# Forgetting attention and a tanh-shrink MLP on one core: batch 0's scores in two-bank groups, a selector tile, and unread matmuls in slot 1

## The chip, the cores and the metric

The kernel runs on one core of one Trainium2 chip. The metric is the device time of one execution in microseconds (us), the median over the runs shown. Engines are named as in the profile: PE (TensorE matmul), PEld (its weight load), DVE (VectorE), ACT (ScalarE), POOL (GpSimd), SP (SyncE, which here only issues DMAs).

## The reference

Causal attention with a forget gate for 8 batches of 8 heads (576 tokens, head width 64), then an MLP on the 4608 tokens of width 512, with hidden width 2048:

```python
scores = scale * np.matmul(q, k.transpose(0, 1, 3, 2))
log_f = np.log(np.clip(f, 0.0001, 1.0))
cum = np.cumsum(log_f, axis=-1)
decay = cum[:, :, :, None] - cum[:, :, None, :]
scores = np.where(causal, -1000000000.0, scores + decay)
attn = softmax(scores)            # max, exp, sum + 1e-09
x = matmul(attn, v)               # heads side by side: (4608, 512)
h = x @ w_in
return (h - np.tanh(h)) @ w_out
```

## The kernel before

**Pairs and slots.** Attention goes by pairs of heads, four pairs to a batch, 32 in all. A slot is the work around one pair: the scores of that pair, the values of the pair before it, the transposes of q and k of the next pair. Scores stand with the key tile on the partitions, so that they are `QT`/`KT` products and need no transpose. A head's scores are three tiles of up to 512 columns (a PSUM bank); the two heads share a small fourth one, tile 3. Head 0 has tiles 0, 1, 2 and head 1 has tiles 4, 5, 6. `GROUPS` names tiles that share a two-bank buffer and one exponential: group 0 is tiles 0 and 1, group 1 is tiles 2 and 4, group 2 is tiles 5 and 6, group 3 is tile 3.

**Decay.** `QT` and `KT` have 64 rows of data and three rows more: the running sum of log f enters the score matmul through these rows, which DMAs on SP's queue fill (`load_aug`, `const_rows`). Head 0 of batch 0 comes before these DMAs land, and so has its sums by selectors: two extra matmuls, one with `pick[:, 0:1]` (minus one at the two rows of head 0 in `cc`), one with `pick[:, 1:2]` against `cqs`. The code calls such a tile `direct`. A causal edge is one more matmul of 128 columns (`neg16`, `tri16`) in batch 0 and the first pair of batch 1; later an affine select on POOL.

**Order of the work.** All five engines run in the order in which the code issues their instructions. The first five slots follow hand-written lists (`FIRST`). A list's words: a bare number is so many `spin` matmuls of 512 columns into a bank that nobody reads; `q`/`k` with a number are six transposes of the q or k of the pair so many ahead, and the copies of them into `QT`/`KT`; `s` is one score tile, `g` a group; `va`/`vb` are the values of the two heads of the pair before (30 matmuls; after `vb` DVE computes the reciprocals and `xn`); `y` and `x` turn a finished `xn` into `XR` (five transposes on PE and one DVE copy in batch 0, DMA transposes later); `p` and `r` are DVE memsets of paddings (`pads`, `later_rows`; the second also issues DMAs); `h` and `m` are the first MLP steps; `c` issues DMAs.

**PSUM.** While the slots of batch 0 run, the eight banks are: two for `av` (values, and the unread matmuls), one `tr` and one `t2`, which the transposes of q, k and x take in turn (`t_bank`: odd calls `t2`, even calls `tr`), and four for scores: four buffers of one bank in slot 0, then two buffers of two banks. From slot 4 on there are `av`, `tr`, two score banks and three MLP banks.

**Later slots.** From slot 5 on, `att_items` lists a slot's tiles 0 to 6 with what goes between them (loads, transposes of the next pair behind tile 2 and tile 5, values of the pair before behind tile 1), and MLP steps are spread evenly among them. An MLP step of the first kind is four matmuls, a tanh on ACT and an add on DVE (`gt`, line 417, at times with two `sm` adds); of the second kind it is eight matmuls of a product of seven (a Strassen-like scheme, so that `wsum` forms differences of `w_out`'s blocks on DVE, `WT1` to `WT4`). For 512 tokens there are 16 of the first and 14 of the second. The transposes' copies run on DVE ("VV"), in slots 7 and 8 on ACT ("AA").

Of the kernel before, what the change touches and what calls it, by code (L numbers as in the profile page):

```python
# [8 lines left out]
FP32 = mybir.dt.float32  # L9
# [8 lines left out]
FAR = 3  # L18
# [4 lines left out]
def kernel(  # L23
# [104 lines left out]
    tri16 = WS[3].rearrange("p k e -> p (k e)")[:, 640:768]  # L128
    ones16 = cst.tile([P, S], FP16)
    minus16 = WS[2].rearrange("p k e -> p (k e)")[0:2 * H, 0:S]  # L130
    pick = cst.tile([P, 2], FP16)
    cc = cst.tile([P, S], FP16)
    chi, clo = cc[0:NH, :], cc[NH:2 * NH, :]
    cqs = cst.tile([P, S], FP16)
# [29 lines left out]
    nc.vector.memset(neg16, 0.0)  # L164
    nc.vector.memset(tri16, 0.0)
    nc.vector.memset(QT[0][D:D + 3, 0, :], 0.0)
    load_qk(qn, q, 0, 4, 6)
    load_qk(kn, k, 0, 4, 6)
    nc.gpsimd.affine_select(out=neg16, in_=neg16, compare_op=ALU.not_equal,
# [109 lines left out]
    def trans(b, c, src, dst, engs):  # L279
        pn, g3 = S // NT6, NT6 // 2  # L280
        t16 = t_bank().bitcast(FP16)[:, 0:2 * S // 2].rearrange("p (a g n) -> p a g n", a=2, g=g3)
        for a in range(2):
            for g in range(g3):
                nc.tensor.transpose(out=t16[:, a, g, :], in_=src[b % 2][:, 2 * c + a, 2 * g:2 * g + 2, :],  # L284
                                    identity=id16[0:pn, 0:pn])
        for a0, an in ((0, 1), (1, 1)) if len(engs) > 2 else ((0, 2),):
            for e in range(2):
                h0 = 2 * c + a0
                to = dst[b % 2][0:D, h0:h0 + an, 0:S].rearrange("d a (g e p) -> d a g e p", g=g3, e=2)[:, :, :, e, :]
                of = t16[e * D:(e + 1) * D, a0:a0 + an, :, :]  # L290
                if engs[2 * a0 + e] == "A":
                    nc.scalar.activation(out=to, in_=of, func=AF.Copy)
                else:
                    nc.vector.tensor_copy(out=to, in_=of)  # L294
            if a0 == 0 and engs == "AAAA":
                cum_q()

    def head_tiles(a):
        return [[(a, 0, 0, 512, 0)],
# [12 lines left out]
    def scores(b, c, tis, how):  # L312
        n2 = len(tis)
        banks = POOLS["s"].tile([P, 2 if how == "group" else 1, UW], FP32, tag="sc", name="ps")
        if tis[0] == LAST:
            eb = EL[(b * NPAIR + c) % 3].rearrange("p (o w) -> p o w", o=1)
        else:
            g, o = PLACE[tis[0]]
            if b == 0:
                if o == 0:  # L320
                    EB[(b, c, g)] = gtp.tile([P, 2, UW], FP16, tag="gt", name="e2")
                eb = EB[(b, c, g)][:, o:o + n2, :]
            else:
                eb = aex.tile([P, 1, UW], FP16, tag="e", name="e")
        for i, ti in enumerate(tis):
            ps, e = banks[:, i, :], eb[:, i, :]
            for a, j, i0, n, col in TILES[ti]:
                h = 2 * c + a
                edge = min(P, n) if how != "late" and i0 == j * P else 0
                direct = b == 0 and h == 0  # L330
                kn_ = min(P, S - j * P) if direct else P
                nc.tensor.matmul(out=ps[:, col:col + n], lhsT=KT[b % 2][0:D + 3, h, j * P:(j + 1) * P],  # L332
                                 rhs=QT[b % 2][0:D + 3, h, i0:i0 + n], start=True, stop=not (edge or direct))
                if direct:
                    nc.tensor.matmul(out=ps[0:kn_, col:col + n], lhsT=cc[:, j * P:j * P + kn_],
                                     rhs=pick[:, 0:1].to_broadcast([P, n]), start=False, stop=False)
                    nc.tensor.matmul(out=ps[:, col:col + n], lhsT=pick[:, 1:2].to_broadcast([P, P]),
                                     rhs=cqs[:, i0:i0 + n], start=False, stop=not edge)
                if edge:
                    nc.tensor.matmul(out=ps[:, col:col + edge], lhsT=neg16, rhs=tri16[:, 0:edge],  # L340
                                     start=False, stop=True)
# [6 lines left out]
        nc.scalar.activation(out=eb[:, :, lo:hi], in_=banks[:, 0:n2, lo:hi], func=AF.Exp, scale=qscale)  # L348
# [141 lines left out]
    for u in range(NU):  # L490
        mlp += [[(mlp1, u, ft)] for ft in turns]
        mlp += [[(product, u, n, g)] for n, g in ((1, 0), (1, 1), (2, 0), (6, 0), (6, 1), (2, 1))]
        mlp += [[(product, u, n, g)] for n in (5, 7, 3, 4) for g in range(2)]
    for at, n in ((NFT, 0), (NFT + 1, 2), (NFT + 3, 1), (NFT + 5, 3)):
        mlp[at] += [(wsum, n, 0, K2 // 2), (wsum, n, K2 // 2, K2)]

    STEPS = [0]

    def step():
        for fn, *args in mlp[STEPS[0]]:  # L500
            fn(*args)
        STEPS[0] += 1

    FIRST = [["8", "q0", "k0", "5", "s0", "s1", "q1", "s2", "k1", "p", "s4", "s5", "q2", "s6", "s3"],
# [4 lines left out]

    def first_slot(p):  # L510
        here = pairs[p]
        before = pairs[p - 1] if p else None
        for what in FIRST[p]:
            kind, arg = what[0], what[1:]
            if what == "m":
                step()
            elif kind == "h":
                mlp1_part(0, turns[int(arg)], 0, NCH - 1)
            elif kind == "s":
                scores(*here, (int(arg),), "one")  # L520
            elif kind == "g":
                scores(*here, GROUPS[int(arg)], "group")
            elif kind in "qk":
                trans(*pairs[p + int(arg)], *((qn, QT) if kind == "q" else (kn, KT)),
                      "VV" if p or arg != "0" else "AAAA" if kind == "q" else "VVVV")
                if what == "k0":
                    load_aug(0, 1)
            elif kind == "v":
                values(*before, 0 if arg == "a" else 1)
            elif kind == "r":  # L530
                later_rows()
            elif kind == "p":
                pads()
            elif kind == "c":
                const_rows(0, 0, 1)
                load_aug(2)
            elif kind == "x":
                turn(*before)
            elif kind == "y":
                turn(*pairs[p - 2])  # L540
            else:
                spin(int(what))

    def att_items(p):
# [67 lines left out]
```

## Time and profile before

| what | us |
|---|---|
| median of 3 runs | 350.78 (350.43 to 350.84) |
| the profiled execution, its own time | 350.38 |
| its span in the profile | 348.7 |
| PE busy | 334.7 |
| DVE busy | 253.3 |
| ACT busy | 220.2 |
| POOL busy | 176.9 |

The profile shows one execution. A row of the timeline has the start, the duration, the engine, the line, the operation, the tiles with shapes, the count, and in brackets how long the engine had been idle before it and what released it. A row of the windows has the stretch, its length, then the busy time and number of instructions of each engine, then the TensorE clock that was granted (1.00 is full speed), the DMA share and GB/s. Matmul durations include the way through the array, so that successive matmuls overlap: the spacing of starts is what a matmul costs.

### The profile page before, as it was taken

How to read it: one execution, taken by the hardware profiler on the slowest of the kernel's cores; microseconds unless marked ns; L12 is line 12 of the kernel's file. 1: busy time of each engine (PE TensorE's matmuls, PEld its weight loads, DVE VectorE, ACT ScalarE, POOL GpSimd, SP SyncE). 2: the span in 40 equal slices, each digit the busy share in tenths (PEclk: the TensorE clock that was granted, in tenths of full speed). 3: DMA queues.
4: the chain of work that ended last, by engine and by line, in shares of the span. 5: the costliest groups of instructions: out<-in, count | busy, mean ns of one | idle time of the engine just before them, and what ended most of it. 6: DMA issues, size and time to landing. Idle time of an engine off the chain costs nothing.

```text
span 348.7 us, 8658 instructions
## 1 busy us (share of the span) xinstructions
PE 334.7 (96%) x3295; PEld 234.1 (67%) x3295; DVE 253.3 (73%) x523; ACT 220.2 (63%) x412; POOL 176.9 (51%) x322
## 2 busy tenths in 40 slices
PE   7898998998999999999999999999999999999996
PEld 2585556774578656887886568756887786487475
DVE  7576889819896589748984889388937863873872
ACT  6564876777765786568756875588558843623631
POOL 8967179875277726774667457753222220500500
PEclk9989999999999999999999999999999999999999
DMA  9999999999589998999699979994122013003003
GB/s 100 145 181 176 195 180 136 131 168 208 83 65 119 179 149 80 116 168 175 65 120 141 180 87 110 156 168 74 47 83 46 19 34 122 0 12 111 3 0 122
DMA packets 169560, 38.82 MB, mean 111 GB/s; under 512 B 155906, under 2 KB 169454, under 8 KB 169518
## 3 DMA queue, kind: packets, MB, share of 16 engines
q0 software_dynamic: 116576, 18.36, 87.2%
q1 hardware_dynamic: 52942, 19.90, 29.1%
q8 instruction: 26, 0.43, 0.6%
q14 instruction: 16, 0.13, 0.1%
HBM read 36.85 MB, written 9.44 MB: 133 GB/s over the span
## 4 chain that ended last, share of the span: by engine, by line
PE 78%; DVE 12%; DMA 4%; ACT 3%; issue 2%; SPq 1%; POOL 0%; DVEq 0%; ACTq 0%; POOLq 0%
PE mb L404 29%; PE px L452 16%; PE mb L452 12%; PE ps L332 11%; PE av L369 7%; DVE gt L417 4%; DMA out_dram<-ost 2%; DVE KT L294 2%; DVE sm L431 2%; DVE xn L377 1%; DMA kn<-in_k_dram 1%; ACT th L411 1%; ACT e L348 1%; PE t L284 1%; DVE QT L294 1%
## 5 line engine op out<-in xcount | busy, mean ns | idle before, releaser
L404 PE MATMUL mb<-XR,win 128*128 128x512 f16 (+4 forms) x704 | 141.6, 340 | 1.0 <-DVE gt L417 0.7
L348 ACT ACTIVATE e<-ps 128x512 f16<-128x512 f32 (+1 forms) x183 | 109.3, 617 | 28.2 <-PE ps L332 15.7
L411 ACT ACTIVATE th<-mb 128x512 f32<-128x512 f32 x144 | 86.3, 600 | 50.8 <-PE mb L404 46.5
L417 DVE TENSOR_TENSOR gt<-mb,th 128x512 f16<-128x512 f32 x144 | 97.1, 686 | 25.2 <-ACT th L411 24.4
L359 POOL TENSOR_SCALAR_AFFINE_SELECT e<-e 128x128 f16<-128x128 f16 x162 | 59.7, 372 | 104.5 <-ACT e L348 103.9
L404 PEld LDWEIGHTS <-win 128*128 128x128 f16 x704 | 61.8, 97 | 49.2 <-issue 2.8
L332 PE MATMUL ps<-QT,KT 67*128 67x64 f16 (+4 forms) x384 | 75.4, 279 | 4.3 <-DVE KT L294 1.4
L452 PEld LDWEIGHTS <-gt 128*128 128x128 f16 x576 | 53.8, 97 | 10.9 <-DVE gt L417 1.1
L332 PEld LDWEIGHTS <-KT 67*128 67x128 f16 x384 | 36.3, 99 | 26.4 <-DVE KT L294 3.4
L452 PEld LDWEIGHTS <-sm 128*128 128x128 f16 x432 | 40.4, 97 | 7.2 <-DVE ws L266 0.6
L452 PE MATMUL mb<-ws,gt 128*128 128x256 f16 x288 | 36.4, 272 | 0.0
L482 DVE TENSOR_TENSOR ost<-mb,part 128x512 f32<-128x512 f32 x25 | 17.1, 685 | 25.9 <-PE mb L404 6.8
L369 PEld LDWEIGHTS <-e 128*128 128x128 f16 x896 | 32.9, 98 | 3.7 <-DVE xn L377 0.9
L369 PE MATMUL av<-vn,e 128*128 128x65 f16 x896 | 34.4, 194 | 0.7 <-DVE xn L377 0.7
L469 ACT ACTIVATE part<-px 128x512 f32<-128x512 f32 x24 | 14.3, 597 | 30.1 <-PE px L452 30.1
L452 PE MATMUL px<-ws,sm 128*128 128x256 f16 x256 | 31.6, 272 | 0.0
L113 POOL DMA_DIRECT2D vn<-in_v_dram x32 | 28.7, 905 | 2.4 <-issue 1.9
L377 DVE TENSOR_TENSOR xn<-av,rs 128x640 f16<-128x640 f32 x32 | 26.4, 824 | 1.1
L431 POOL TENSOR_TENSOR sm<-gt 128x512 f16<-128x512 f16 x4 | 4.6, 1152 | 36.3 <-DVE gt L417 36.3
L94 POOL DMA_DIRECT2D qn<-in_q_dram x25 | 21.8, 872 | 1.5 <-issue 1.4
L94 POOL DMA_DIRECT2D kn<-in_k_dram x25 | 21.4, 854 | 1.2 <-issue 0.9
L452 PE MATMUL mb<-wout,gt 128*128 128x256 f16 x160 | 21.4, 272 | 0.0
(83 smaller groups left out, 302.6 us busy)
## 6 DMA issues: line engine op xcount, KB each, us to landing
out_dram<-ost SPq DMA_DIRECT2D x34, 256.0 KB
vn<-in_v_dram POOLq DMA_DIRECT2D x32, 128.0 KB, 5.9
qn<-in_q_dram POOLq DMA_DIRECT2D x20, 128.0 KB, 3.8
kn<-in_k_dram POOLq DMA_DIRECT2D x20, 128.0 KB, 4.7
win<-in_moe_w_in_dram POOLq DMA_DIRECT2D x4, 512.0 KB, 8.6
wout<-in_moe_w_out_dram POOLq DMA_DIRECT2D x2, 1024.0 KB, 16.3
qn<-in_q_dram POOLq DMA_DIRECT2D x10, 144.0 KB, 7.4
kn<-in_k_dram POOLq DMA_DIRECT2D x10, 144.0 KB, 7.1
```

Of the source, the lines that this page charges most:

```text
L94: nc.gpsimd.dma_start(out=dst[b % 2][0:pn, n, :].rearrange("p (h d) -> p h d", h=H), in_=src[b, :, n * P:n * P + pn, :].rearrange("h p d - ...
L113: nc.gpsimd.dma_start(out=vn[b % 2][:, n, h0:h1, 0:D], in_=v[b, h0:h1, n * P:(n + 1) * P, :].rearrange("h p d -> p h d"))
L332: nc.tensor.matmul(out=ps[:, col:col + n], lhsT=KT[b % 2][0:D + 3, h, j * P:(j + 1) * P], rhs=QT[b % 2][0:D + 3, h, i0:i0 + n], start=True ...
L348: nc.scalar.activation(out=eb[:, :, lo:hi], in_=banks[:, 0:n2, lo:hi], func=AF.Exp, scale=qscale)
L359: nc.gpsimd.affine_select(out=view, in_=view, compare_op=ALU.is_ge, fill=0.0, base=0, pattern=pat, channel_multiplier=-1)
L369: nc.tensor.matmul(out=av[:, a, ib, :], lhsT=E.pop((b, c, a, j, ib)), rhs=vn[b % 2][:, j, 2 * c + a, 0:D + 1], start=(j == 0), stop=(j == ib))
L377: nc.vector.tensor_tensor(out=xn.rearrange("p i (a d) -> p a i d", a=2), in0=av[:, :, :, 0:D], in1=rs.to_broadcast([P, 2, NJ, D]), op=ALU. ...
L404: nc.tensor.matmul(out=hps[:, o:o + n], lhsT=win[:, ci, ft * P:(ft + 1) * P], rhs=XR[:, ci, t:t + n], start=(ci == 0), stop=(ci == NCH - 1))
L411: nc.scalar.activation(out=th, in_=hps, func=AF.Tanh, scale=-1.0)
L417: nc.vector.tensor_tensor(out=GT[(u, ft)], in0=hps, in1=th, op=ALU.add)
L452: nc.tensor.matmul(out=ps[:, g * E2:(g + 1) * E2], lhsT=left(k), rhs=right[:, k, :], start=(first and (g == 0 or last) and k == 0), stop=( ...
L482: nc.vector.tensor_tensor(out=ost, in0=ps, in1=PART.pop((u, {2: 1, 7: 5, 4: 6}[n])), op=ALU.add)
```

## The change

Five things are changed.

- **Slot 0.** The copies of pair 0's transposed q and k are taken out of `trans` and put into `begin`: head 0's q halves go through ACT, then the cumulative row `cqs`, one half of k through DVE and the other through ACT, then the small exponential that calls the Exp table (it stood right behind the Ln before), and the four halves of head 1 through DVE. Three unread matmuls follow in place of five. The scores run as groups 0, 1, 2, 3 in the two-bank buffers. Tile 4, head 1's first, is `direct` too, with a new selector column `pick[:, 2:3]` and a column of the identity.
- **Slot 1.** Two unread matmuls stand before group 3, three behind group 2; both groups move ahead of the values; group 0 of pair 2 (`n`) moves from slot 2 in between the two heads' values; `later_rows` goes last.
- **Slots 2 to 4.** Some words change places: in slot 2 `k1` goes ahead of `y`, in slot 3 `vb` goes ahead of `k1`, in slot 4 `x` goes ahead of `h2` and `q1`, and `k1` ahead of an `m`.
- **Later slots.** The next pair's q and k are transposed behind tiles 1 and 4 rather than 2 (in slot 7: 3) and 5.
- **`wsum`.** Each of the four differences of weights is split over two MLP steps, from steps 14, 16, 19 and 22 on, where all of it stood at steps 16, 17, 19 and 21.

```diff
-    pick = cst.tile([P, 2], FP16)
+    pick = cst.tile([P, 3], FP16)
+    first = cst.tile([1, 1], FP32)
...
+    nc.vector.scalar_tensor_tensor(out=pick[:, 2:3], in0=id16[:, 1:2], scalar=-1.0, in1=id16[:, NH + 1:NH + 2],
+                                   op0=ALU.mult, op1=ALU.subtract)
...
-    first = cst.tile([1, 1], FP32)
-    nc.scalar.activation(out=first, in_=lf[0:1, 0:1], func=AF.Exp)
...
-        for a0, an in ((0, 1), (1, 1)) if len(engs) > 2 else ((0, 2),):
+        for e, eng in enumerate(engs):
+            copy(b, c, dst, t16, 0, 2, e, eng)
+        return t16
...
+    def begin():
+        tq, tk = BEGIN["q"], BEGIN["k"]
+        for e in range(2):
+            copy(0, 0, QT, tq, 0, 1, e, "A")
+        cum_q()
+        copy(0, 0, KT, tk, 0, 1, 0, "V")
+        copy(0, 0, KT, tk, 0, 1, 1, "A")
+        nc.scalar.activation(out=first, in_=lf[0:1, 0:1], func=AF.Exp)
+        for dst, t16 in ((KT, tk), (QT, tq)):
             for e in range(2):
...
+                copy(0, 0, dst, t16, 1, 1, e, "V")
...
-                direct = b == 0 and h == 0
+                direct = b == 0 and (h == 0 or h == 1 and ti == 4)
+                minus, plus = (pick[:, 0:1], pick[:, 1:2]) if h == 0 else (pick[:, 2:3], id16[:, 1:2])
                 kn_ = min(P, S - j * P) if direct else P
...
+                rows = D if direct and h else D + 3
+                nc.tensor.matmul(out=ps[:, col:col + n], lhsT=KT[b % 2][0:rows, h, j * P:(j + 1) * P],
+                                 rhs=QT[b % 2][0:rows, h, i0:i0 + n], start=True, stop=not (edge or direct))
...
-    for at, n in ((NFT, 0), (NFT + 1, 2), (NFT + 3, 1), (NFT + 5, 3)):
-        mlp[at] += [(wsum, n, 0, K2 // 2), (wsum, n, K2 // 2, K2)]
+    for at, n in ((NFT - 2, 0), (NFT, 2), (NFT + 3, 1), (NFT + 6, 3)):
+        for o in range(2):
+            mlp[at + o] += [(wsum, n, o * K2 // 2, (o + 1) * K2 // 2)]
...
-    FIRST = [["8", "q0", "k0", "5", "s0", "s1", "q1", "s2", "k1", "p", "s4", "s5", "q2", "s6", "s3"],
-             ["g0", "g1", "k1", "g3", "va", "r", "vb", "q2", "g2"],
-             ["g0", "y", "va", "g1", "k1", "vb", "g3", "q2", "g2"],
-             ["g0", "y", "va", "g1", "k1", "vb", "g3", "g2"],
-             ["c", "va", "s0", "y", "vb", "s1", "h0", "h1", "q1", "h2", "x", "s2", "m", "s3", "m", "s4", "m", "k1", "s5", "m", "s6", "m"]]
+    FIRST = [["8", "q0", "k0", "b", "3", "g0", "q1", "g1", "k1", "p", "q2", "g2", "g3"],
+             ["g0", "g1", "k1", "2", "g3", "g2", "3", "va", "n", "vb", "q2", "r"],
+             ["g1", "k1", "y", "va", "vb", "g3", "q2", "g2"],
+             ["g0", "y", "va", "g1", "vb", "k1", "g3", "g2"],
+             ["c", "va", "s0", "y", "vb", "s1", "h0", "h1", "x", "h2", "q1", "s2", "m", "s3", "m", "s4", "k1", "m", "s5", "m", "s6", "m"]]
...
+            elif kind == "b":
+                begin()
+                load_aug(0, 1)
+            elif kind == "n":
+                scores(*pairs[p + 1], GROUPS[0], "group")
...
-            if ti in (3 if p == 2 * NPAIR - 1 else 2, 5) and after and after[0] < FAR:
-                dst, src = (KT, kn) if ti == 5 else (QT, qn)
+            if ti in (1, 4) and after and after[0] < FAR:
+                dst, src = (KT, kn) if ti == 4 else (QT, qn)
...
-            with tc.tile_pool(name="ps_one", bufs=4, space=PSUM) as POOLS["s"]:
-                first_slot(0)
             with tc.tile_pool(name="ps_two", bufs=2, space=PSUM) as POOLS["s"]:
-                for p in range(1, NPAIR):
+                for p in range(NPAIR):
                     first_slot(p)
```

More of the change, by code (lines that the diff above doesn't have):

```diff
@@ L285, in trans, with copy @@
                                     identity=id16[0:pn, 0:pn])
-        for a0, an in ((0, 1), (1, 1)) if len(engs) > 2 else ((0, 2),):
-            for e in range(2):
[L288 to L296, printed above, removed]
+        for e, eng in enumerate(engs):
+            copy(b, c, dst, t16, 0, 2, e, eng)
+        return t16
+    def copy(b, c, dst, t16, a0, an, e, eng):
+        h0 = 2 * c + a0
+        to = dst[b % 2][0:D, h0:h0 + an, 0:S].rearrange("d a (g e p) -> d a g e p", g=NT6 // 2, e=2)[:, :, :, e, :]
+        of = t16[e * D:(e + 1) * D, a0:a0 + an, :, :]
+        if eng == "A":
+            nc.scalar.activation(out=to, in_=of, func=AF.Copy)
+        else:
+            nc.vector.tensor_copy(out=to, in_=of)
+    BEGIN = {}
+    def begin():
[7 more added lines that the diff above has]
+        for dst, t16 in ((KT, tk), (QT, tq)):
+            for e in range(2):
+                copy(0, 0, dst, t16, 1, 1, e, "V")
     def head_tiles(a):
@@ L329, in scores @@
                 edge = min(P, n) if how != "late" and i0 == j * P else 0
-                direct = b == 0 and h == 0
+                direct = b == 0 and (h == 0 or h == 1 and ti == 4)
+                minus, plus = (pick[:, 0:1], pick[:, 1:2]) if h == 0 else (pick[:, 2:3], id16[:, 1:2])
                 kn_ = min(P, S - j * P) if direct else P
-                nc.tensor.matmul(out=ps[:, col:col + n], lhsT=KT[b % 2][0:D + 3, h, j * P:(j + 1) * P],
-                                 rhs=QT[b % 2][0:D + 3, h, i0:i0 + n], start=True, stop=not (edge or direct))
+                rows = D if direct and h else D + 3
+                nc.tensor.matmul(out=ps[:, col:col + n], lhsT=KT[b % 2][0:rows, h, j * P:(j + 1) * P],
+                                 rhs=QT[b % 2][0:rows, h, i0:i0 + n], start=True, stop=not (edge or direct))
                 if direct:
                     nc.tensor.matmul(out=ps[0:kn_, col:col + n], lhsT=cc[:, j * P:j * P + kn_],
-                                     rhs=pick[:, 0:1].to_broadcast([P, n]), start=False, stop=False)
-                    nc.tensor.matmul(out=ps[:, col:col + n], lhsT=pick[:, 1:2].to_broadcast([P, P]),
+                                     rhs=minus.to_broadcast([P, n]), start=False, stop=False)
+                    nc.tensor.matmul(out=ps[:, col:col + n], lhsT=plus.to_broadcast([P, P]),
                                      rhs=cqs[:, i0:i0 + n], start=False, stop=not edge)
@@ L523, in first_slot @@
             elif kind in "qk":
[L524 to L527, printed above, removed]
+                BEGIN[kind] = trans(*pairs[p + int(arg)], *((qn, QT) if kind == "q" else (kn, KT)),
+                                    "VV" if p or arg != "0" else "")
             elif kind == "v":
                 values(*before, 0 if arg == "a" else 1)
+            elif kind == "b":
[3 more added lines that the diff above has]
+                scores(*pairs[p + 1], GROUPS[0], "group")
             elif kind == "r":
```

## The prediction

> **What bounds the kernel now.** I read the page's busy times first, then the windows, then each engine's timeline for the first 100 us.
>
> ```profile
> PE 334.7 (96%) x3295; PEld 234.1 (67%) x3295; DVE 253.3 (73%) x523; ACT 220.2 (63%) x412; POOL 176.9 (51%) x322
> ...
> 36.00:40.00 4.00, 3.72 (x28) 1.83 (x26) 3.63 (x7) 3.96 (x9) 0.00 (x0) 1.00 1.80 183
> 50.00:55.00 5.00, 4.52 (x36) 2.40 (x33) 4.82 (x11) 3.32 (x7) 3.93 (x8) 1.00 3.27 139
> ...
> 110.00:130.00 20.00, 19.97 (x178) 12.44 (x177) 12.39 (x23) 14.57 (x29) 12.11 (x26) 1.00 1.66 167
> ```
>
> PE is the bound as a whole, but not everywhere. From 110 us on it is full (19.97 of 20) and DVE is not (12.39), so what is won or lost ahead of that reaches the end whole. In 36 to 40 us ACT is full (3.96 of 4), and then DVE (4.82 of 5 in 50 to 55): PE's waits there are DVE's queue, and a copy moved within that queue only moves the wait. Almost the whole change lies ahead of 70 us.
>
> The second reading is the clock, in windows of 3.41 us laid so that one falls on the slow stretch. PE's busy time stands behind the length, the granted clock behind the bracket.
>
> ```profile
> 13.70:17.11 3.41, 2.31 (x26) 1.00 2.53 148
> 17.11:20.53 3.42, 3.39 (x47) 0.50 1.93 172
> ...
> 27.35:30.77 3.42, 2.45 (x51) 1.00 2.16 170
> ```
>
> One window ran at half speed: 3.4 us in which PE did 1.7 us of work. The window ahead of it had PE busy 2.31 of 3.41; one with 2.45 had no such sequel. The threshold lies near 2.4, if this count is the right one. The Trainium skill (TensorE: Matmul & The Clock Gate, Part 1) has the clock halved after an idle window of about 3.4 us: by that rule no order of slot 1 could be slowed, and five unread matmuls would be 1.1 us spent for nothing. The trace disagrees: the window ahead of the slow one was 68% busy.
>
> **Slot 0.** PE's timeline, then DVE's:
>
> ```profile
> 7.22 2.33 PE L271 MATMUL spin<-ones 128*128 128x512 f16 x5
> 9.34 0.63 PE L332 MATMUL ps<-QT,KT 67*128 67x512 f16 x1
> 10.20 0.43 PE L337 MATMUL ps<-cqs,pick 128*128 128x512 f16 x1
> ...
> 13.63 0.22 PE L340 MATMUL ps<-ws 128*128 128x128 f16 x1
> 14.30 0.20 PE L332 MATMUL ps<-QT,KT 67*128 67x64 f16 x1 [0.46 <-DVE KT L194]
> 15.25 0.38 PE L332 MATMUL ps<-QT,KT 67*128 67x512 f16 x1 [0.36 <-ACT el L348]
> 15.46 0.22 PE L340 MATMUL ps<-ws 128*128 128x128 f16 x1
> 16.42 0.42 PE L284 MATMUL t<-id,kn 96*128 96x96 f16 x6
> ```
> ```profile
> 7.46 1.28 DVE L294 COPY KT<-t 64x288 f16<-64x288 f16 x4
> 12.73 0.92 DVE L294 COPY KT<-t 64x576 f16<-64x576 f16 x2
> 13.98 0.27 DVE L194 MEMSET KT<- 64x256 uint32 x1
> ```
>
> A matmul of 512 columns costs 0.43 at first (two from 9.34 to 10.20) and 0.22 later (15.25 to 15.46); I put the change at 10.29, two windows ahead of 17.11. The first score stood behind five unread matmuls, which end with DVE's four quarters of K (8.74). Now head 0's K is there at about 7.9 (one quarter of 0.32 on DVE, one on ACT at the same time), three unread matmuls end at 7.22 + 3 x 0.43 = 8.50, and the scores start there, 0.84 earlier. At the slow clock that is 0.42 of work. The selectors of tile 4 add two matmuls of 512 columns: 0.43. Both cancel, and group 2 ends at 13.7 as its tiles did. The Exp table's loading moves behind ACT's copies, where ACT waits for scores till about 11; the new selector column on DVE fits ahead of the scan, which waits for ACT: both nothing, or 0.1 if that cover goes. Group 3 waits for a padding memset. Tile 4 now stands ahead of the k transposes, so their copy and the memset come 0.27 later (14.57). But the buffers no longer change at the end of the slot: slot 1 starts at 15.0 instead of 15.25. **0.25 ahead.** The window 13.70 to 17.11 has PE waiting only from 13.85 to 14.57, so busy 2.65 with the two unread matmuls of slot 1 in it: no slow window at 17.11.
>
> **Slots 1 and 2.**
>
> ```profile
> 21.86 0.30 PE L332 MATMUL ps<-QT,KT 67*128 67x320 f16 x1
> 22.48 0.42 PE L284 MATMUL t<-id,kn 96*128 96x96 f16 x6
> 22.74 0.59 PE L369 MATMUL av<-vn,e 128*128 128x65 f16 x14
> 23.19 0.20 PE L332 MATMUL ps<-QT,KT 67*128 67x64 f16 x1
> 24.37 0.38 PE L332 MATMUL ps<-QT,KT 67*128 67x512 f16 x1
> 30.08 0.44 PE L387 MATMUL t<-id,xn 128*128 128x128 f16 x5
> 30.35 0.59 PE L369 MATMUL av<-vn,e 128*128 128x65 f16 x14
> ```
> ```profile
> 16.06 1.94 ACT L348 ACTIVATE e<-ps 128x1024 f16<-128x1024 f32 x2 [0.86 <-PE ps L332]
> ```
> ```profile
> 17.80 0.27 DVE L200 MEMSET KT<- 67x256 uint32 x1
> 18.52 0.12 DVE L202 MEMSET vn<- 128x80 f16 x1
> 19.20 0.17 DVE L375 TENSOR_SCALAR rs<-av 128x10 f32<-128x10 f32 x1 [0.55 <-PE av L369]
> 19.65 0.82 DVE L377 TENSOR_TENSOR xn<-av,rs 128x640 f16<-128x640 f32 x1
> ```
>
> Prices by the starts, at full clock: a group of two tiles 0.62 (group 0 0.55, by columns), six transposes 0.26, a head's values 0.45, `y` 0.27. `xn` with its reciprocals is 1.28, `later_rows` 0.84, a pair's copy 0.92. Laid down in the new order, groups 0 and 1 and k end at 16.43, and two unread matmuls at 16.86. The exponentials run 0.25 earlier than their row, 15.81 to 17.75, the first to 16.83: the two matmuls fill that wait. Group 3 ends 17.02; group 2 waits for the second exponential, 17.82, and ends 18.43. The three unread matmuls come behind it, where nothing is waited for: the values need only pair 0's exponentials, of which the last ends at about 15.5. So 0.64 of PE time is spent. Values a end 19.53, group 0 of pair 2 20.08, values b 20.53, q 20.80; slot 2's group 1 and k end 21.68. In the old order group 1 and k end at 22.74 with `y` and one head's values (0.72) done besides, so like work ended at 22.02: PE is 0.34 ahead.
>
> There a new wait comes. `y` is the ninth call of `t_bank` and takes `t2`, which holds the transposed q of pair 3 (seventh call; before, `y` was the eighth and took `tr`). DVE copies that q only behind pair 0's `xn`, which starts at 20.73 where it started at 19.20. `xn` ends 22.0, the copy 22.85: PE stands from 21.68 to 22.9, and all of slot 2's values are queued behind `y`, to 24.16. DVE runs `later_rows` (0.84) and the copy of k to 24.6; slot 2's q transposes wait for that copy, and slot 2 ends at 25.61 where it ended at 24.37. **1.24 behind.**
>
> **Slots 3 and 4.**
>
> ```profile
> 29.34 0.59 PE L369 MATMUL av<-vn,e 128*128 128x65 f16 x14 [0.70 <-DVE xn L377]
> 33.82 0.45 PE L387 MATMUL t<-id,xn 128*128 128x128 f16 x5 [0.37 <-DVE QT L294]
> ```
> ```profile
> 34.65 0.60 ACT L348 ACTIVATE e<-ps 128x512 f16<-128x512 f32 x1 [2.77 <-PE ps L340]
> ```
>
> These waits are slack. On DVE, `XR` (0.46, half a pair's copy) and pair 1's `xn` follow to 26.45, which slot 3's `y` waits for; values a, group 1 and values b bring PE to 28.30, and pair 2's `xn` ends at 29.75. Slot 4's first values wait for it (the 0.70 of before), and start at 29.81: only 0.47 behind. Then tile 0 to 30.54; `y` waits for `tr`, whose k copy is behind `xn` (30.67), to 31.01; values b, tile 1, `h0` and `h1` to 33.04; `x` without its wait of 0.37, `h2`, q, and tile 2 ends at 34.56. Its exponential starts at 34.76, against 34.65. As ACT has no gap from that row to 39 us, this exponential passes the start on: **0.1 behind.** The k transposes one MLP step earlier let DVE close a gap of 0.35 (its 3.63 of 4): **0.25 ahead** on DVE, the bound from there.
>
> **Slots 5 to 10.** The waits that the earlier transposes and the split differences aim at (31 to 120 us):
>
> ```profile
> PE ps L332 <- DVE KT L294: 1.4, 3, 0.7
> PE t L284 <- DVE QT L294: 0.9, 3, 0.5
> ...
> PE mb L452 <- DVE ws L266: 0.5, 1, 0.5
> PE ps L332 <- ACT KT L292: 0.4, 1, 0.4
> ```
> ```profile
> 46.71 0.91 DVE L294 COPY KT<-t 64x576 f16<-64x576 f16 x2
> 57.96 1.38 DVE L266 TENSOR_TENSOR ws<-wout 128x1024 f16<-128x1024 f16 x2
> 78.67 0.69 DVE L482 TENSOR_TENSOR ost<-mb,part 128x512 f32<-128x512 f32 x1 [6.83 <-PE mb L404]
> ```
>
> They sum to 3.2, the most there is. In slots 5 and 6 DVE is full: the copies move ahead, but each add that they pass comes later by 0.91, and half of the first difference (0.69) lands ahead of slot 6's K copy, so that slot 7 may even start 0.5 later. I give these slots nothing beyond the 0.25. In slot 7 DVE gets past the differences, and the copies of slots 7 and 8 are ACT's: the waits for `ws` and for ACT's K go, and PE begins slot 8 some 0.25 + 0.9 = 1.15 ahead. The last difference now stands at steps 22 and 23, ahead of pair 7's `xn` on DVE, so that `xn`, and on SP's queue the output's DMA behind its two transposes, come only 0.65 earlier. For that DMA DVE stands 6.83 us, so it comes free 0.65 earlier. Of the waits behind it (the longest for KT, the shorter ones for QT) I take back 0.45. **Sum: 0.65 + 0.45 = 1.1.** The profiled execution took 350.38, a span of 348.7 and 1.7 around it; less 1.1 it is 349.28. The median is 0.40 above it, and I predict against the median: 350.78 - 1.1 = 349.7.
>
> **Rivals.** *The clock falls after all, two windows later.* In my schedule the window 20.53 to 23.94 has PE busy to 21.84 (with the last matmul's way out) and from 22.9 on, 2.35: between the 2.31 that was followed by half speed and the 2.45 that was not. Of the 2.35, three sets of transposes (0.26, 0.26, 0.27) are 0.8. If transposes don't count, 1.55 remains, against 2.05 in the window that slowed the clock (one set, 16.42) and 2.18 in the one that did not (one set, 30.08). Then 23.94 to 27.35 runs at half speed: slot 4's third tile comes 0.95 later, slot 5 starts some 0.6 behind, and the gains of slots 7 to 10 little more than pay for it: 350.7. The Trainium skill (TensorE: Matmul & The Clock Gate, Part 4) says that transposes don't count as busy PE in the same way; the two windows above fit either count.
>
> *Slower: DVE becomes the bound of slots 2 to 4.* The chain is a pair's `xn`, the copy of q, the memsets, the copy of k, `XR`, the next `xn`, and each copy releases one of PE's two transpose banks. If each of its six links costs 0.3 more than the rows say, slot 4's third tile comes out 2 us late; the later gains of 0.9 do not pay: 350.78 + 2.0 - 0.9 = 351.9. It decides from pair 2's `xn` ending after 30.5 on. For it: DVE would do nothing for 3 us up to 20.73, and that slack is gone. Against: ACT idled 2.77 ahead of 34.65.
>
> *The waits go whole.* If q is copied soon enough that slot 2's bank wait doesn't show, slots 7 to 10 keep the 1.15 and what slot 2 saves (about 1): 348.7.
>
> **How the numbers follow.** Forecast 0.45, clock 0.27, slower 0.22, whole 0.06. About 0.2% (0.7 us) is what a measurement of this kernel tells from no change, so faster is below 350.1 and slower above 351.5. The forecast, with 0.6 either way, gives 0.37 to faster and 0.08 to the same; the clock 0.05, 0.16 and 0.06; the whole 0.06 to faster, the slower 0.22 to slower: 0.48, 0.24, 0.28. The range, 348.7 to 351.9, goes from the best case to the middle of the slower one.
>
> **What would show it.** Right: the first score at 8.5, slot 1's first group near 15.0, a granted clock of 1.00 from 17.1 to 20.5, slot 2's five transposes with a wait of over 1 us for DVE, the exponential of slot 4's third tile near 34.8, no wait for `ws`, PE 1.2 ahead around 65. The clock rival: 0.50 in 23.9 to 27.4. The slower one: pair 2's `xn` ending after 30.5 and ACT idle till 36. I am wrong if slot 4's third tile is off by more than 1 us either way, or if slots 5 and 6 get faster although DVE is full.

## The result, and the profile after

The changed kernel takes 351.66 us (350.40 to 353.85, 14 runs) against 350.60 for the kernel before (349.66 to 351.18, 14 runs): a ratio of 1.0031, 95% interval 1.0016 to 1.0045. It is slower, by 0.16 to 0.45%, where 1.1 us faster was forecast. The profiled execution took 352.38, with a span of 350.7.

The busy times and the windows of the kernel after, with the columns of the prediction's windows:

```profile
PE 333.4 (95%) x3300; PEld 232.8 (66%) x3300; DVE 254.7 (73%) x525; ACT 220.1 (63%) x408; POOL 177.2 (51%) x322
```
```profile
13.70:17.11 3.41, 2.81 (x30) 1.93 (x31) 2.46 (x7) 2.88 (x5) 3.41 (x6) 1.00 2.74 143
17.11:20.53 3.42, 3.36 (x55) 2.46 (x55) 0.34 (x2) 1.87 (x3) 3.42 (x5) 1.00 1.98 167
20.53:23.94 3.41, 2.21 (x50) 1.82 (x47) 3.16 (x9) 1.32 (x3) 2.38 (x3) 1.00 1.26 198
23.94:27.35 3.41, 3.15 (x51) 2.53 (x52) 2.96 (x8) 2.12 (x3) 0.81 (x2) 1.00 2.32 159
...
75.00:80.00 5.00, 3.95 (x55) 2.70 (x53) 0.16 (x1) 2.35 (x5) 2.38 (x5) 1.00 2.08 159
80.00:85.00 5.00, 2.92 (x19) 1.45 (x19) 4.44 (x9) 1.64 (x4) 2.58 (x6) 1.00 1.72 186
110.00:130.00 20.00, 19.95 (x185) 13.01 (x183) 12.56 (x27) 13.86 (x28) 11.72 (x24) 1.00 1.61 170
```

The granted clock is 1.00 in all of them. PE is full from 110 us on, as it was. The new thing is 75 to 85 us: PE is busy 3.95 and 2.92 of 5, with DVE all but idle in the first half (0.16 of 5) and nearly full in the second (4.44). The same two windows of the kernel before:

```profile
75.00:80.00 5.00, 4.43 (x59) 3.18 (x59) 1.26 (x4) 2.97 (x7) 2.94 (x6) 1.00 2.40 171
80.00:85.00 5.00, 4.69 (x27) 2.08 (x25) 4.89 (x10) 3.64 (x8) 3.51 (x7) 1.00 1.74 232
```

PE is busy 2.25 us less there than before (4.43 + 4.69 less 3.95 + 2.92). PE's timeline after, from the first matmul of slot 9 to the first Strassen product of the next row block of the MLP:

```profile
73.46 0.38 PE L350 MATMUL ps<-QT,KT 67*128 67x512 f16 x1
...
80.59 1.02 PE L422 MATMUL mb<-XR,win 128*128 128x512 f16 x4 [1.64 <-DVE ost L500]
...
83.32 1.02 PE L422 MATMUL mb<-XR,win 128*128 128x512 f16 x4 [1.49 <-DVE gt L435]
...
87.63 0.61 PE L350 MATMUL ps<-QT,KT 67*128 67x512 f16 x3 [0.86 <-DVE KT L298]
...
101.38 1.04 PE L470 MATMUL px<-wout,gt 128*128 128x256 f16 x8
```

And the same two ends before:

```profile
74.59 0.38 PE L332 MATMUL ps<-QT,KT 67*128 67x512 f16 x1
...
99.15 1.04 PE L452 MATMUL px<-wout,gt 128*128 128x256 f16 x8
```

At slot 9 the changed kernel is 1.13 us ahead; at the product it is 2.23 behind. Between them DVE's queue stands at one instruction, the fourth add into the output tile `ost`. That tile has two buffers, so the fourth add waits until the second one has been written to memory. DVE's timeline after, and then before:

```profile
70.13 0.69 DVE L500 TENSOR_TENSOR ost<-mb,part 128x512 f32<-128x512 f32 x1 [0.39 <-PE ps L350]
79.84 0.69 DVE L500 TENSOR_TENSOR ost<-mb,part 128x512 f32<-128x512 f32 x1 [9.02 <-DMA out_dram<-ost]
80.45 0.91 DVE L298 COPY QT<-t 64x576 f16<-64x576 f16 x2
...
81.85 0.82 DVE L395 TENSOR_TENSOR xn<-av,rs 128x640 f16<-128x640 f32 x1
82.59 2.09 DVE L435 TENSOR_TENSOR gt<-mb,th 128x512 f16<-128x512 f32 x3
```
```profile
79.72 0.82 DVE L377 TENSOR_TENSOR xn<-av,rs 128x640 f16<-128x640 f32 x1
80.47 1.28 DVE L417 TENSOR_TENSOR gt<-mb,th 128x512 f16<-128x512 f32 x2
81.66 0.91 DVE L294 COPY QT<-t 64x576 f16<-64x576 f16 x2
```

DVE comes free at 79.84, where it was 78.67. And what stands next in its queue has changed: before, `xn` and the adds came first and the q copy behind them; now the earlier transposes put the copy ahead, and the adds that PE's MLP steps wait for start at 82.59 where they started at 80.47. SP's timeline shows when the awaited output was issued, before and after:

```profile
72.79 0.54 SPq L483 DMA_DIRECT2D out_dram<-ost  x1
```
```profile
72.40 0.53 SPq L501 DMA_DIRECT2D out_dram<-ost  x1
```

It was issued 0.39 earlier and released DVE 1.17 later. The difference of the two spans, 2.0, is then 1.17 from the release and 0.83 from what follows it (350.7 - 79.84 = 270.86 against 348.7 - 78.67 = 270.03).

### The profile page after: what moved, and what is told of

Its sections match the earlier page's. It is cut to its first block, busy times and chain, and to the rows that moved or that the text cites. A ratio compares the mean times of both kernels' runs of the same rounds, so it can differ in the third digit from the quotient of the medians.

```text
span 350.7 us, 8666 instructions
## 1 busy us (share of the span) xinstructions
PE 333.4 (95%) x3300; PEld 232.8 (66%) x3300; DVE 254.7 (73%) x525; ACT 220.1 (63%) x408; POOL 177.2 (51%) x322
## 4 chain that ended last, share of the span: by engine, by line
PE 81%; DVE 10%; ACT 4%; DMA 3%; issue 1%; SPq 0%; ACTq 0%; DVEq 0%
PE mb L422 30%; PE px L470 16%; PE mb L470 14%; PE ps L350 12%; PE av L387 7%; DVE gt L435 3%; DMA out_dram<-ost 2%; ACT e L366 2%; DVE KT L298 2%; DVE sm L449 1%; DVE xn L395 1%; ACT th L429 1%; DMA ws<-in_f_dram 1%; PE t L285 1%; DVE QT L298 1%
## 5 line engine op out<-in xcount | busy, mean ns | idle before, releaser
L387 PEld LDWEIGHTS <-e 128*128 128x128 f16 x896 | 31.9, 97 | 2.7 <-issue 0.3
L387 PE MATMUL av<-vn,e 128*128 128x65 f16 x896 | 33.6, 193 | 0.1
L393 DVE TENSOR_SCALAR rs<-av 128x10 f32<-128x10 f32 x32 | 5.2, 162 | 24.7 <-PE av L387 24.5
```

Of the source, the lines that this page charges most:

```text
L387: nc.tensor.matmul(out=av[:, a, ib, :], lhsT=E.pop((b, c, a, j, ib)), rhs=vn[b % 2][:, j, 2 * c + a, 0:D + 1], start=(j == 0), stop=(j == ib))
```

## The experiments

The rows above name three suspects: the output's DMA, the q copy ahead of `xn`, and the new start, whose loss could be hidden by that wait. Each ratio is against runs of the kernel before on the same chip; the medians of those were 350.57 to 350.76.

| what runs | buffers of `ost` | us | ratio to before (95%) |
|---|---|---|---|
| before, 350.60 | 2 | 350.60 | 1 |
| new start only | 2 | 350.76 | 0.9999 (0.9988 to 1.0010) |
| new later slots only | 2 | 352.48 | 1.0049 (1.0030 to 1.0067) |
| the change | 2 | 351.66 | 1.0031 (1.0016 to 1.0045) |
| before | 3 | 348.24 | 0.9935 (0.9914 to 0.9956) |
| new start only | 3 | 350.50 | 0.9994 (0.9981 to 1.0008) |
| new later slots only | 3 | 348.42 | 0.9938 (0.9917 to 0.9958) |
| the change | 3 | 350.17 | 0.9971 (0.9957 to 0.9985) |

"Start" is the first five slots, "later slots" the transposes behind tiles 1 and 4 with the split differences of `wsum`.

**A third output buffer, in both kernels.**

```diff
+    osp = ctx.enter_context(tc.tile_pool(name="osp", bufs=3))
-        ost = tmp.tile([P, DM], FP32, tag="ost", name="ost") if half != 1 else PART.pop((u, n, "ost"))
+        ost = osp.tile([P, DM], FP32, tag="ost", name="ost") if half != 1 else PART.pop((u, n, "ost"))
```

Changed kernel:

> The changed kernel with three output buffers (ost) instead of two, nothing else. Theory A (the output buffer): the loss arises at 70.8 to 79.8 us, where DVE stands 9.02 us for the DMA out of an output buffer, and PE then stands 1.64 and 1.49 for what DVE has not done. With a third buffer the wait goes whole, PE keeps the 1.1 us that it is ahead at slot 9, and the time falls from 351.7 to 349.3 (348.8 to 349.8). Rival B (the start): slots 0 to 4 with five unread matmuls and the bank wait of 1.07 us make it slower; then the third buffer changes little: 351.3 to 351.7. Rival C (the copies): the copies of q and k, issued earlier, stand ahead of the adds on DVE; then about half comes back, 350.5.

Kernel before:

> The kernel before with three output buffers, nothing else; a control for the third buffer by itself. In the kernel before DVE stands 6.83 us at the same place, and PE afterwards about 1.2 us in all. Theory A: the third buffer gives it some 0.8 us, 349.8 (349.4 to 350.3), less than it gives the changed kernel, which is then the faster of the two. Rivals B and C: no more than 0.3 us, 350.3 to 350.6.

Measured 350.17 and 348.24. Both expectations missed. DVE's timelines, changed kernel and kernel before, each with the third buffer:

```profile
76.53 0.69 DVE L501 TENSOR_TENSOR ost<-mb,part 128x512 f32<-128x512 f32 x1 [4.89 <-PE mb L471]
```
```profile
74.96 0.69 DVE L483 TENSOR_TENSOR ost<-mb,part 128x512 f32<-128x512 f32 x1 [5.01 <-PE mb L453]
```

The add now waits 4.9 to 5.0 us for the product that it adds, and no longer for a DMA. In the kernel before, the row quoted in the prediction named PE's line 404 as the releaser of this wait; its length without the DMA, and its releaser (line 453 here, the products), point to the DMA. The wait had been worth 2.4 us to the kernel before and 1.5 to the changed one, and without it the changed kernel is 1.9 slower. So part of what the change costs had been hidden in the wait.

**Slot 9's transposes back behind tiles 2 and 5.**

```diff
-            if ti in (1, 4) and after and after[0] < FAR:
-                dst, src = (KT, kn) if ti == 4 else (QT, qn)
+            at = (2, 5) if p == 2 * NPAIR + 1 else (1, 4)
+            if ti in at and after and after[0] < FAR:
+                dst, src = (KT, kn) if ti == at[1] else (QT, qn)
```

> The changed kernel, with the transposes of slot 9 alone (behind the output's wait) put back behind tiles 2 and 5; all other slots as changed. On DVE xn and the adds then stand ahead of the copy of q when the wait ends. Theory A: the wait of 9 us stays, and only the copy's 0.9 us can come back: 350.8 (350.5 to 351.2). Rival C (the copies are the loss): 1.5 us and more come back, 350.1 or less. Rival B: no change, 351.7.

350.74, ratio 0.9997 (0.9984 to 1.0011): 0.9 less than the change, as expected. DVE's timeline:

```profile
78.89 0.69 DVE L500 TENSOR_TENSOR ost<-mb,part 128x512 f32<-128x512 f32 x1 [6.48 <-PE mb L422]
...
79.94 0.82 DVE L395 TENSOR_TENSOR xn<-av,rs 128x640 f16<-128x640 f32 x1
...
81.87 0.91 DVE L298 COPY QT<-t 64x576 f16<-64x576 f16 x2
```

`xn` is the first thing behind the wait again, and the copy follows. Not all of the 0.9 need be the order, because the wait also ended earlier in this profile (78.89 against 79.84). The two spans differ by 1.7 us: 0.95 is the release, and 0.75 lies behind it (349.0 - 78.89 = 270.11 against 270.86), where the order is what differs.

**The new start alone**, two buffers, then three:

```diff
-            if ti in (1, 4) and after and after[0] < FAR:
+            if ti in (3 if p == 2 * NPAIR - 1 else 2, 5) and after and after[0] < FAR:
...
-    for at, n in ((NFT - 2, 0), (NFT, 2), (NFT + 3, 1), (NFT + 6, 3)):
+    for at, n in ((NFT, 0), (NFT + 1, 2), (NFT + 3, 1), (NFT + 5, 3)):
```

> Slots 0 to 4 as changed, the later transposes and the differences of weights as before. Theory A: the start as such costs nothing, since the third tile's exponential of slot 4 comes at 34.74 against 34.65: 350.4 (350.0 to 350.8). Rival B (the start is the loss): 351.5 or more. Rival C: 350.6, as before.

> Slots 0 to 4 as changed, the later slots and the differences of weights as before, and three output buffers, so that what the start costs is no longer swallowed by the output's wait. To be held against the kernel before with three buffers (348.24). Theory D (the start is slower at the same clock): in the profile of that kernel, whose clock was full from 6.9 us on, slot 4's third tile has its exponential at 32.64, with the changed start at 34.74 at the same clock: about 1.5 to 2.0 slower, 349.8 to 350.3. Rival E (the start is even, as the two first profiles say, 34.65 and 34.74, and the loss is in the later slots): 348.2.

350.76 and 350.50, the second a little above what was expected. With the DMA's wait the new start costs nothing that can be seen; without it, it costs 2.3 (350.50 against 348.24). The clock is not the reason: among the runs with a mean granted clock of 1.00 alone, the kernel before with three buffers took 347.73 to 348.10 (three runs) and the new start with three 349.31 to 350.71 (four runs). That is the answer to where the loss was hidden: with two buffers the add is released by a DMA at about the same time, whether DVE comes early or late.

**The new later slots alone**, three buffers, then two. The edit is the reverse of the last diff, made in the kernel before:

> Slots 0 to 4 as before, the later transposes and the split differences as changed, and three output buffers. Theory D: the later slots gain some 0.4 (from slot 4's third tile to the end 312.96 in the changed kernel with three buffers against 313.36 in the kernel before with three): 347.8 (347.4 to 348.3). Rival E: 349.8 or more.

> Slots 0 to 4 as before, the later transposes and the split differences as changed, two output buffers as in both kernels: the missing fourth of the square (before, start alone 350.76, this, both 351.66). Theory H (the output's wait swallows what comes ahead of it, and the copy of q ahead of xn and the adds costs 0.9 behind it): 351.5 (351.1 to 351.9), about as the whole change. Rival I (the loss is in the start, and only together with the later slots): 350.3 to 350.8.

348.42 and 352.48. With three buffers they bring nothing (348.24 without them). The profiles with three buffers show a gain and a loss. From the exponential of slot 4's third tile to the add into `ost` the new later slots take 0.8 us less (41.54 against 42.32 with the old start, 40.99 against 41.83 with the new), and from that add to the end 0.5 and 0.9 more. With two buffers they cost 1.9. SP's and DVE's timelines with two buffers:

```profile
70.56 0.53 SPq L483 DMA_DIRECT2D out_dram<-ost  x1
```
```profile
79.11 0.69 DVE L482 TENSOR_TENSOR ost<-mb,part 128x512 f32<-128x512 f32 x1 [9.87 <-DMA out_dram<-ost]
79.71 0.91 DVE L294 COPY QT<-t 64x576 f16<-64x576 f16 x2
```

Here the output was issued 2.23 earlier than in the kernel before and released DVE 0.44 later: 8.6 us from issue to release, against 5.9. Being early at that wait brings nothing. The expectation had the sign and half of the size. Behind the release the two-buffer profiles fall into two groups. To the end of the span it is 269.9 us (start alone), 270.0 (before) and 270.1 (slot 9 back) where `xn` comes first, and 270.9 (the change), 271.1 (transposes later, see below) and 271.6 (this kernel) where the copy of q does. So the order costs 0.8 to 1.7 us there; why it isn't the same in the three was not tried apart.

**What holds the output's DMA.** The loads of k for batch 3 run beside it, and so do the DMA transposes of q on SP's queue. POOL's timeline in the changed kernel, the first and the last of the five loads (128 KB each, the last 64):

```profile
66.79 0.90 POOL L94 DMA_DIRECT2D kn<-in_k_dram  x1
...
72.56 0.69 POOL L94 DMA_DIRECT2D kn<-in_k_dram  x1
```

The loads, and then the transposes, were moved five tiles later in the changed kernel, with two buffers:

```diff
-            at_tile(p0, n, lambda b=b, n=n: load_block(kb, k, b, n))
+            at_tile(p0, n + (5 if b == FAR else 0), lambda b=b, n=n: load_block(kb, k, b, n))
```

> The changed kernel with two output buffers; batch 3's five k loads on POOL's queue (issued at 67 to 74 us) five tiles later, so that the second output of the first 512 tokens, issued at about 72.4, has fewer loads beside it. Theory J (the loads on the same 16 DMA engines stretch the output's DMA, 7.4 us from issue to landing): it lands 1.5 to 3 us earlier, DVE's wait of 9 us falls to 6 to 7.5, and the time to 350.2 (349.8 to 350.8). Rival K (the DMA transposes on SP's own queue stretch it): no change, 351.4 to 351.9.

```diff
-            at_tile(p0, 4 + n, lambda b=b, n=n: turn_block(TQ, qb, b, n))
+            at_tile(p0, (9 if b == FAR else 4) + n, lambda b=b, n=n: turn_block(TQ, qb, b, n))
```

> The changed kernel with two output buffers; batch 3's five transposes of q on SP's queue (from 73 us on) five tiles later, so that none is issued between the outputs. Rival K (SP's transposes stretch the output's DMA): it lands 1.5 to 3 us earlier, and the time is 350.2 (349.8 to 350.8). Theory J (the loads do): no change, 351.4 to 351.9.

350.12 (0.9991, interval 0.9973 to 1.0009) and 351.26 (1.0027, 1.0015 to 1.0040). DVE's timeline with the loads later, then with the transposes later:

```profile
76.48 0.69 DVE L500 TENSOR_TENSOR ost<-mb,part 128x512 f32<-128x512 f32 x1 [4.89 <-PE mb L470]
```
```profile
78.19 0.69 DVE L500 TENSOR_TENSOR ost<-mb,part 128x512 f32<-128x512 f32 x1 [7.48 <-DMA out_dram<-ost]
```

With the loads out of the way the output, issued at 72.94, is out before the product is there, and the kernel takes what it takes with a third buffer (350.17). So it is the loads that hold it. The transposes have a smaller part at most: the release comes 1.65 earlier than in the changed kernel, with the DMA still the releaser, and the 0.4 us of time is within what these runs can tell.

**What the start loses**, with three buffers: the three unread matmuls behind group 2 left out; `q2` ahead of the values; both. The first diff is against the change, as are the others, of which only the new line is shown.

```diff
-             ["g0", "g1", "k1", "2", "g3", "g2", "3", "va", "n", "vb", "q2", "r"],
+             ["g0", "g1", "k1", "2", "g3", "g2", "va", "n", "vb", "q2", "r"],
```

> The changed kernel with three output buffers and without the three unread matmuls behind group 2 in slot 1 (two are left ahead of group 3). Against 350.17. Theory D: they cover no wait and hold up the values and pair 0's xn by 0.64, and with it the whole chain on DVE: 349.5. Rival F (they keep the clock up): a slow window of 3.41 us appears between 20 and 28 us in most runs, and the time is 350.2 to 351.

```diff
+             ["g0", "g1", "k1", "2", "g3", "g2", "3", "q2", "va", "n", "vb", "r"],
```

> The changed kernel with three output buffers, and in slot 1 the transposes of pair 3's q put ahead of the values instead of behind them, so that DVE copies it while it is idle (3.34 us up to 20.16) and slot 2's y finds its bank free. Against 350.17. Theory D: the wait of 1.07 ahead of y goes, pair 0's XR and pair 1's xn come about 0.9 earlier, slot 4's third tile 0.5 to 1.0 earlier: 349.4 (349.1 to 349.9). Rival G (PE's wait only moves to xn, which ends at 21.4): 350.0 or more.

```diff
+             ["g0", "g1", "k1", "2", "g3", "g2", "q2", "va", "n", "vb", "r"],
```

> The changed kernel with three output buffers, without the three unread matmuls behind group 2, and with pair 3's q transposed ahead of slot 1's values: both mends of the start together (349.17 and 349.33 one by one, from 350.17). Theory D: they add up, as the one shortens PE's way to the values and the other takes pair 3's copy off DVE behind xn: 348.3 (347.8 to 348.8), even with the kernel before with three buffers (348.24). Rival: what they have in common is the wait of y, and together they give no more than one: 349.1.

349.17 (0.9953, 0.9932 to 0.9974), 349.33 (0.9956, 0.9940 to 0.9972) and 348.62 (0.9939, 0.9922 to 0.9955). By the medians the unread matmuls cost 1.0 of the 350.17, the bank wait 0.84, both 1.55. One by one, the intervals still overlap that of the 350.17 (0.9957 to 0.9985); together they don't. The profiles bear out both: without the three unread matmuls the exponential of slot 4's third tile stands 1.04 ahead of the changed kernel's 34.74, both at the full clock, and with `q2` ahead of the values `y` no longer waits 1.07 for the bank, but 0.50 for `xn`. ACT's row of the first kernel and PE's row of the second:

```profile
33.70 0.60 ACT L367 ACTIVATE e<-ps 128x512 f16<-128x512 f32 x1 [2.28 <-PE ps L359]
```
```profile
23.53 0.45 PE L406 MATMUL t<-id,xn 128*128 128x128 f16 x5 [0.50 <-DVE xn L396]
```

What is left against the kernel with the old start (348.42) is 0.2, less than these intervals can tell from nothing. Without the three unread matmuls no slow stretch of the clock appears behind them in the profile, and 2 of its 9 runs have a mean clock of 0.995, against 3 of 11 with them. One window of that kernel, PE alone:

```profile
20.00:28.00 8.00, 6.19 (x120) 1.00 1.82 182
```

In its profile the next DMA-fed wait shows up as the output's wait had. PE's waits from 74 to 100 us, with the unread matmuls and then without:

```profile
PE mb L423 <- DMA XR<-xn: 0.3, 1, 0.3
```
```profile
PE mb L423 <- DMA XR<-xn: 1.6, 1, 1.6
```

PE reaches it 1.8 us earlier and stands 1.3 longer. Some 0.8 of the 1.8 is the clock and not the order: in the profile with the unread matmuls, matmuls of 512 columns still started 0.42 apart at 8.33 us, and slot 4's third tile stands at 35.54, against 34.74 for the same start at the full clock.

The lowest median is that of the kernel before with a third output buffer: 348.24, ratio 0.9935 (0.9914 to 0.9956). The new later slots (348.42) and the kernel with both edits of the start (348.62), each with three buffers, can't be told from it.

## Why the prediction was wrong

**Slot 0 and slot 1's front: places near, gains not.** PE's timeline after:

```profile
8.28 0.39 PE L350 MATMUL ps<-QT,KT 67*128 67x512 f16 x1 [0.47 <-ACT KT L296]
8.50 0.38 PE L353 MATMUL ps<-pick,cc 128*128 128x512 f16 x1
...
14.28 0.38 PE L350 MATMUL ps<-QT,KT 67*128 67x512 f16 x1
...
17.02 0.35 PE L350 MATMUL ps<-QT,KT 67*128 67x448 f16 x1 [0.59 <-ACT e L366]
17.64 0.81 PE L272 MATMUL spin<-ones 128*128 128x512 f16 x3
...
22.32 0.45 PE L405 MATMUL t<-id,xn 128*128 128x128 f16 x5 [1.07 <-DVE QT L298]
...
30.37 0.38 PE L350 MATMUL ps<-QT,KT 67*128 67x512 f16 x1 [0.61 <-ACT e L366]
```

The first score was to start at 8.5 and did at 8.28; slot 1 at 15.0 and did at 14.28, because this execution had the full clock from its first score on (0.22 from 8.28 to 8.50), where the prediction laid the slow clock till 10.29. In the profile of the changed kernel with three buffers, whose first matmuls still start 0.42 apart, slot 1 starts at 15.08. But the gains were reckoned against the profile of before, whose clock was lower here. The kernel before with three buffers, at the full clock from its first score on, has that score at 8.14 and slot 1 at 14.35, so that next to nothing is left of the 0.84 and the 0.25. (The prediction also has the five unread matmuls of before end at 8.74; from 7.22 on, with 0.43 each, they end at 9.37.) The stretch at half speed from 17.11 to 20.53 is absent here, as forecast, but that can't be credited to the order: such stretches move between executions, as the last section shows. `y`'s wait for its bank is the "over 1 us" of the prediction (1.07 at 22.32). The wait of 0.61 at 30.37 had not been laid down.

**Slot 4's third tile: right number by luck, wrong reading.** ACT's timeline:

```profile
34.74 0.60 ACT L366 ACTIVATE e<-ps 128x512 f16<-128x512 f32 x1 [2.28 <-PE ps L358]
```

34.74 stands against a forecast of 34.76, and against 34.65 before, hence "0.1 behind". But in the profile of before the matmuls of 512 columns started 0.43 apart up to about 10.3 (the clock column has 1.00 there all the same), and a half-speed window came as well; this one had neither. The kernel before with three buffers, in an execution without such a window, has that exponential at 32.64:

```profile
32.64 0.60 ACT L349 ACTIVATE e<-ps 128x512 f16<-128x512 f32 x1 [2.77 <-PE ps L341]
```

At like clock the new start is some 2 us behind, not 0.1: the prediction took the clock of one execution for a property of the order. The half-speed window alone cost 1.7 us of PE work by its own count. DVE's first row for pair 0's `xn`, in the changed kernel and in the kernel before with three buffers, shows that the loss is already there:

```profile
20.16 0.17 DVE L393 TENSOR_SCALAR rs<-av 128x10 f32<-128x10 f32 x1 [3.34 <-PE av L387]
```
```profile
17.78 0.17 DVE L376 TENSOR_SCALAR rs<-av 128x10 f32<-128x10 f32 x1
```

That is 2.38 later, as PE starts pair 0's values at 18.50 and not at 16.36. The prediction set its 20.73 against 19.20, a row behind the half-speed window's first part, and saw 1.53. Its term for the start (0.1 behind at the tile, 0.25 ahead on DVE) was mis-sized; the runs show 1.75 to 2.3 (350.17 less 348.42, 350.50 less 348.24).

**Slots 5 to 8: right.** No gain in slots 5 and 6 and a K copy behind the first difference were forecast, with slot 7 up to 0.5 later; PE's row is 0.59 later than 56.31 before:

```profile
56.90 0.61 PE L350 MATMUL ps<-QT,KT 67*128 67x512 f16 x3 [0.80 <-DVE KT L298]
```

No wait for `ws` is left, slot 8 starts 0.90 ahead (1.15 forecast) and slot 9 1.13. Here the profiles agree with the schedule, but what is gained up to the output's add is lost again behind it, as the three-buffer profiles above show.

**The step that failed.** "For that DMA DVE stands 6.83 us, so it comes free 0.65 earlier", and "of the waits behind it I take back 0.45". The prediction let the wait's end follow its beginning. The end is when the DMA lands among the loads. In the profiles with two buffers and the loads in place the output was issued and DVE released at 70.56 and 79.11 (later slots alone), 71.95 and 78.19 (transposes later), 72.40 and 79.84 (the change), 72.53 and 79.11 (start alone), 72.79 and 78.67 (before), 73.81 and 78.89 (slot 9 back): 3.25 us of issue, 1.65 of release, and no order between them. So the 0.65 was nothing, and in the changed kernel's profile -1.17. And the 0.45 had the wrong sign: the step did not ask what the moved transposes put next in DVE's queue behind that add. The q copy of 0.91 went ahead of `xn` and the adds. With that order undone in slot 9 the median falls by 0.9 (351.66 less 350.74), and behind the release the order costs 0.8 to 1.7 in the profiles.

**The rivals.** The clock's fall from 23.94 on did not come in this execution (1.00, with 2.21 busy in the window ahead of it: less than the 2.31 that was held to be under the threshold). The slower rival had the right size, at equal clock (2 us at slot 4's third tile), but not the mechanism. DVE's copies cost what the rows said, pair 2's `xn` ended at 29.07 and not after 30.5, and the loss is there when the chain begins: the runs find three unread matmuls (1.0) and the bank wait (0.84), not six links of 0.3. The time that it gave (351.9) lies near the measured one by accident, since with two buffers the start's loss isn't seen. The whole-gain rival fell with the bank wait.

It stays open what places the release within its 1.65 us. The order alone, with its 0.8 to 1.7, could make up the 1.06 us between the medians; what the release adds or takes in the median run, one profile of each kernel doesn't show.

## What to carry to other kernels

Where an engine waits for a DMA, the wait's end need not move with its beginning (here issues 3.25 us apart were released within 1.65 us, in no order): before tuning what comes ahead of it, add a buffer or move the loads beside it, because until then the wait swallows both gains and losses (here 2.3 us of loss). Ask of a moved instruction what it will stand in front of when the queue is released, not only whether it is ready sooner. And before two profiles' rows are compared, compare their clock row by row: the half-speed window in one of them, 1.7 us of PE work, was worth more here than the whole forecast gain.

## What the runs showed of the hardware

**The clock's slow stretches move between executions.** The half-speed window of before, at 17.11, is one of several places. Windows of PE alone: the new start with three buffers, then the change with slot 9's transposes back, then `q2` ahead of the values:

```profile
8.20:11.50 3.30, 3.23 (x18) 0.55 2.24 148
```
```profile
8.80:12.20 3.40, 3.40 (x21) 0.52 2.07 140
```
```profile
15.90:19.20 3.30, 3.30 (x23) 0.50 2.64 150
```

The changed kernel itself had none in its profile, though its first five slots are the same code as those of the first two; 4 of its 14 runs have a mean clock of 0.989 to 0.995, as a run with such a stretch has (0.995 with slot 9's transposes back). The Trainium skill (TensorE: Matmul & The Clock Gate, Part 1) says that the clock's window of about 3.4 us is free-running and doesn't start anew with the kernel. That the slow stretch is 3.3 to 3.4 us long here and stands at four places is in line with it. So the prediction's grid of windows, laid out from one execution, doesn't hold for the next, and what an order of slot 1 does to the clock can't be read from one profile of it. The kernel without the three unread matmuls behind group 2 had no slow stretch from 20 to 28 us either; the two ahead of group 3 were not left out.

**A store beside loads.** In one profile of each, the same 256 KB took from issue to release 5.9 us in the kernel before, 7.4 in the changed one and 8.6 with the new later slots alone; with the five loads moved away, 3.54 at the most (72.94 to 76.48, when the add had its product).
